# Linear attention on pairs of chunks: neighbouring tokens in one partition, 384-byte packets, a new order of work

## The chip, the cores and the metric

The kernel runs on one core of a Trainium2 chip. The metric is the device time of one execution in microseconds (us), lower is better. The engines are TensorE (PE), VectorE (DVE), ScalarE (ACT), GpSimd (POOL) and SyncE (SP); SP only issues transfers here, and 16 DMA engines carry them.

## The reference

Two stages follow one another: a linear attention with a decaying state, and a gated convolution over the whole sequence. B = 4 sequences, H = 8 heads, S = 768 tokens, D = 48 values a head, so 384 channels.

```python
for t in range(S):                                   # per batch and head
    cur = einsum('bhd,bhe->bhde', u[None] * kt, vt)
    y[:, :, t] = einsum('bhd,bhde->bhe', rt, state + cur)
    state = wt[:, :, :, None] * state + einsum('bhd,bhe->bhde', kt, vt)
x = y.transpose(0, 2, 1, 3).reshape(B, S, H * D)
x1, x2, x3 = split(x @ w_proj, 3)                    # w_proj [384, 1152]
x2_conv = irfft(rfft(x2, axis=1) * rfft(filter_fft, axis=0))
out = (x1 * x2_conv * x3) @ w_out                    # [4, 768, 384] float32
```

The inputs `r`, `k`, `v` and `w` are float32 of shape [4, 8, 768, 48], so one token of one head is 192 contiguous bytes.

## The kernel before

Stage one works on 24 chunks of 128 tokens, six for each sequence. A chunk has its 128 tokens in the 128 partitions. Chunks are loaded in groups of one or two (`group`): tiles `wl` (w), `kr` (k and r) and `vl` (v). One load brings one chunk of one input with a packet of 192 bytes for each token and head; 12 of the 24 chunks of v come through POOL's queue and are cast to bf16 on the way.

Per group, ACT takes the logarithm of w (`ln`, tile `lg`), and POOL or DVE makes the term of the current token: `rk` (r times k), `ru` (times u), `rh` (its two halves of 24 added), `cc` (the sum over a head, on DVE), and `vc` (v times that sum).

Per chunk (`first`), the steps are named with the chunk's number behind them: `cs` sums the logarithms over tokens as matmuls with triangular masks; `ex` takes the exponential of both sums; `kq` multiplies them with k and r (DVE); `ph` is the decay over the chunk; `tr` and `qk` turn the scaled k and r so that channels lie in partitions (PE and a copy, or a DMA transpose issued by SP for the last eight chunks); `sc` are the scores; `mt` copies them out of PSUM through the causal mask and `mc` cuts them on POOL where ACT copied them whole; `kv`, `ki` and `su` carry the state on (tile `S`); `yi`, `ys` and `y` add up the output in PSUM: the current token, the state, the scores. `xn` copies the output, `yt` and `xT` turn it.

Stage two (`second`) follows for each sequence: gate projections `p` and `q`, the side projection `xw`, the discrete Fourier transform by matrices `F` (`f`), the product with the filter's spectrum (`u`, `p`), the inverse transform `E` with its sums and differences (`aE` on DVE or `aw` on POOL, then `dE`), the gate (`yE`) and the output projection `o` with its copy `co` and store `so`. The matrices `F` and `mi` are sines that ACT makes with another function table (`trig`, `sin`, `is`, `table`).

The order of the work on all engines is one written-out list, `ORDER`: a line has the step, the engine's letter (P, A, D, G for POOL, S for SP, others for variants, `-` for a step left out) and a PSUM bank where one is needed. Each engine runs its lines in this order, and waits where data or a buffer is not ready. Lines `warm` are matmuls without use that keep PE running.

```python
op(f"l{name}{i}", [SP], lambda ...: nc.sync.dma_start(
    out=t[:, q], in_=x[b, :, rw, :].rearrange("h t d -> t h d")), ...)          # 128 partitions x 8 packets of 192 bytes
nc.tensor.matmul(p[:, par, j, :], qk[f][p0:p0 + D, j, :], qk[f][p0:p0 + D, HP + j, :], ...)   # sc: 8 a chunk, 128 columns
```

Of the kernel before, what the change touches and what calls it, by code (L numbers as in the profile page):

```python
# [20 lines left out]
L = 128  # L21
# [4 lines left out]
DP = 64  # L26
# [10 lines left out]
ADD, DVE2, ACT2, POOL2, FOLD, WIDE = "V", "M", "N", "C", "Q", "X"  # L37

NLW, NLD, NG, NF, NS, NX, NO = 3, 4, 3, 4, 3, 3, 4
CASTS = (2,4,6,8,10,12,)  # L40
NV, NVL = 6, 3
NTURN = 8
# [6 lines left out]
warm 16 4  # L49
first A  # L50
imaps G
smalls D
zeros D
pads D
signs D
lw0 S
lw3 S
kz1 D
ln0 A
maske G  # L60
lw2 S
lr0 S
u S
maskn G smalls
maps G
ang2 D
ia0.0 G
ia1.0 G
maski G
kz0 G pads  # L70
ang1 D
ang0 D
ia2.0 D
cs0 P 2
lk0 S
ln2 A
ex0 A
ew0 -
kq0 D
warm 8 0  # L80
warm 6 1
cs3 P 0
ex3 -
ia2.1 D
kw0 -
lw1 S
ur A
warm 4 5
um P 6
warm 5 5  # L90
tr0 P 4
lk3 S
lr3 S
ew3 X
lr1 S
lk1 S
kz2 G
ph0 A
ub A
ln1 A  # L100
lv0 S
rk0 G ang0
kz3 G kq0
ru0 G
rh0 D
cc0 D
qk0 A
kq3 -
kw3 G rh0
lv2 G cc0  # L110
warm 3 5
cs1 P 5
warm 3 7
sc0 P 3
mt0.1 D
mc0.1 -
lr2 S
lk2 S
vb0 G
vc0 G rh0  # L120
ex1 A
ph3 A
mt0.0 D
ew1 -
lv3 G
warm 3 7
cs2 P 0
warm 4 7
tr3 P 4
ex2 A  # L130
kq1 D
qk3 A
kw1 -
warm 2 7
tr1 P 7
mc0.0 -
rk1 D
ru1 D
rh1 G rk1
qk1 D  # L140
ph1 A
warm 3 2
sc3 P 4
kv0 P 2
su0 D
ew2 -
kq2 D
kw2 -
lv1 S
warm 2 3  # L150
sc1 P 6
yi0 P 2
y0 P
mt1.1 D
lw4 S
mt3.1 -
xn0 A
xa0 -
mt3.0 N
ph2 A  # L160
rk2 D
ru2 D
rh2 G rk2
vb1 A
tr2 P 3
warm 3 2
ki1 P 5
warm 2 2
kv1 P
lw5 S  # L170
lk4 S
lr4 S
qk2 A
ln3 A
mt1.0 D
cc1 D
yt0 P 2
lr5 S
lk5 S
lv5 S  # L180
warm 3 4
sc2 P 0
su1 D
warm 1 3
ki2 P 5
kv2 P
cc2 D
su2 D
cs4 P 6
ex4 A  # L190
wproj1 G
mc3.1 -
ki3 P 4
kv3 P
mt2.1 A
mc1.1 -
ia0.1 G
vc1 D
xT0 D
warm 2 3  # L200
yi1 P 2
ys1 P
vc2 G
mt2.0 D
mc1.0 -
y1 P
ew4 -
su3 D
mc2.1 G mt1.0
kq4 D  # L210
mc2.0 -
cs5 P 0
xn1 A
ex5 A
warm 1 4
yi2 P 3
ys2 P
y2 P
kw4 -
kq5 D  # L220
ew5 -
lw7 S
ph4 A
xn2 A
tr4 P 6
xa1 -
xa2 -
kw5 -
qk4 D
yt1 P 3  # L230
tr5 P 2
yi3 P 6
qk5 D
yt2 P 4
ph5 A
wproj0 G kq4
mc3.0 C
lv4 S
xT2 D
ys3 P  # L240
lr7 S
y3 P
xn3 D
sc4 P 4
mt4.0 D
xa3 -
trig A
sin2 A
rk3 G qk4
ru3 G qk5  # L250
warm 1 0
yt3 P 7
xT1 D
mt4.1 A
ia1.1 G mt4.0
warm 3 0
sc5 P 5
mt5.1 -
lw6 S
mt5.0 M  # L260
xw0.0 P 0
rh3 D
cc3 D
vb3 G rh3
sin1 A
vc3 G mt5.0
ki4 P 2
cxw0.0 D
xT3 A
warm 1 3  # L270
xw0.2 P 6
sin0 A
kv4 P
is A
cxw0.2 D
su4 D
warm 5 4
p0.2.0 P 5
p0.0.0 P 0
table A  # L280
lr6 S
lk6 S
lk7 S
mc4.1 G
filt S
lw8 S
lw9 S
cp0.0.0 D
yi4 P 6
yi5 P 2  # L290
ys5 P
lv7 G cxw0.2
mc5.0 -
mc5.1 -
ys4 P
y5 P
lk9 S
lk8 S
mc4.0 -
y4 P  # L300
xn4 D
if1 A
ln4 A
xn5 A
lv8 S
cs6 P 0
xa5 -
yt5 P 3
if0 A
ex6 A  # L310
lr9 S
xa4 -
yt4 P 2
xT5 D
xT4 D
cs7 P 6
ew6 -
kq6 D
ex7 A
ew7 -  # L320
xw0.4 P 2
lr8 S
kq7 D
ph6 A
cxw0.4 A
sd0.1.0 D
kw7 -
sd0.0.0 D
rk4 G
p0.2.1 P 4  # L330
cp0.2.1 A
ph7 A
kw6 -
lw10 S
p0.0.1 P 0
tr7 P 3
qk7 D
fsd0 D
fsd1 D
tr6 P 7  # L340
ru4 D
cp0.0.1 A
qk6 A
cp0.2.0 A
lv9 S
f0.2 P 0
cf0.2 A
sc6 P 6
mt6.1 -
mc6.1 -  # L350
mt6.0 N
f0.0 P 4
sc7 P 2
cf0.0 A
warm 2 0
h1 P 0
ln5 A
lv6 G sd0.1.0
h2 P 6
rh4 G fsd1  # L360
mt7.1 -
mt7.0 M
mc7.0 -
hc1 A
mc7.1 -
cc4 D
h0 P 2
hc2 A
kv6 P 4
hg1 D  # L370
hg2 D
hc0 A
cs8 P 0
su6 D
mc6.0 C
vc4 G
warm 2 5
yi6 P 6
y6 P
ex8 A  # L380
ew8 -
hg0 D
xn6 A
yi7 P 4
ys7 P
y7 P
xn7 A
xa7 -
xa6 -
cs9 P 6  # L390
kq8 D
yt6 P 3
ki7 P 2
kv7 P
su7 D
wproj2 G
yt7 P 4
xT7 D
ex9 A
xT6 A  # L400
kq9 D
kw8 -
rk5 G
ph8 A
ru5 D
rh5 D
cc5 D
ew9 -
tr8 P 5
ki8 P 2  # L410
qk8 A
ph9 A
vb5 G xT7
vc5 G
xw1.0 P 0
cxw1.0 A
kw9 -
tr9 P 3
qk9 A
kv8 P  # L420
sc8 P 4
su8 D
mt8.1 -
lw11 S
f0.1 P 0
ki9 P 6
kv9 P
mt8.0 M
if2 A
lk10 S  # L430
lk13 S
mc8.0 -
cf0.1 A
sc9 P 2
su9 D
q0.2.1 P 7
lr10 S
mt9.0 N
lk11 S
lr11 S  # L440
mt9.1 -
mc9.1 -
q0.0.1 P 5
lr13 S
yi9 P 0
q0.2.0 P 4
yi8 P 2
xq0.0.1 -
u10.0 D
lw12 S  # L450
ys9 P
ln6 A
ys8 P
cq0.0.1 D
lw13 S
mc8.1 -
y8 P
lv11 G su9
mc9.0 C
warm 5 2 192  # L460
y9 P
cs10 P 5
lr12 S
lv12 S
xq0.2.1 -
u00.0 D
xq0.2.0 -
xn8 A
xn9 A
q0.0.0 P 2  # L470
cq0.2.0 D
cq0.2.1 D
xq0.0.0 -
xa8 -
lk12 S
lv10 G
rk6 G
cq0.0.0 D
xa9 -
gq0.0.0 -  # L480
yt9 P 4
ex10 A
xT9 A
ru6 D
kq10 D
yt8 P 7
xT8 A
cs11 P 0
ex11 A
if3 A  # L490
kq11 D
warm 1 4
xw1.2 P 2
ew10 -
kw10 -
lk15 S
lv13 S
rh6 G ru6
cc6 D
ph10 A  # L500
lr15 S
gq0.2.0 -
lw15 S
lr14 S
p1.2.0 P 4
tr10 P 7
p1.0.0 P 5
cxw1.2 A
qk10 A
ew11 -  # L510
kw11 -
ph11 A
cp1.2.0 A
cp1.0.0 A
tr11 P 2
q1.0.0 P 0
ki10 P 3
sc10 P 4
xq1.0.0 -
ln7 A  # L520
p0.0 D
lw14 S
mt10.1 A
gq0.0.1 -
qk11 D
sc11 P 6
kv10 P
lv15 G
mt11.0 A
vc6 G  # L530
mc10.1 G kq11
mc11.0 G qk11
q1.2.0 P 2
xq1.2.0 -
cq1.0.0 D
mt10.0 D
mt11.1 D
cs12 P 0
rk7 G qk11
ru7 G  # L540
yi10 P 4
ex12 A
ew12 -
su10 D
lv19 G qk11
ys10 P
mc10.0 -
y10 P
lv14 G
mc11.1 -  # L550
cs13 P 6
gq0.2.1 -
cq1.2.0 D
kq12 D
xn10 A
ex13 A
yi11 - 2
ys11 P
y11 P
lk14 S  # L560
xn11 V
E0.0 P 4
kq13 D
ew13 -
kw13 -
ph12 A
gq1.2.0 -
vb7 A
xa10 -
kw12 -  # L570
tr12 P 0
lw17 S
lw16 S
rk8 G
cE0.0 A
aE0.0.1 D
ru8 G
yt10 P 1
E0.1 P 2
xT10 D  # L580
aE0.0.0 D
aw0.0.0 -
qk12 A
ph13 A
xa11 -
cE0.1 A
kv12 P 1
su12 D
aE0.1.0 D
tr13 P 7  # L590
E0.2 P 4
qk13 A
cE0.2 A
aE0.1.1 D
aw0.1.1 -
yt11 P 0
ki13 P 1
kv13 P
lk16 S
aw0.1.0 -  # L600
rh7 D
sc13 P 2
ln8 A
aw0.0.1 -
xT11 D
su13 D
sc12 P 6
mt12.0 N
aE0.2.0 D
aE0.2.1 D  # L610
mt13.1 D
mc13.1 -
mc12.0 C rh7
lv16 S
lw19 S
p1.0.1 P 0
mt12.1 -
cs14 P 4
xw1.4 P 6
dE0.0.1 -  # L620
mt13.0 D
q1.0.1 P 2
cp1.0.1 A
p1.2.1 P 1
cc7 D
ex14 A
kq14 D
ew14 -
kw14 -
tr14 P 0  # L630
cxw1.4 A
ln9 A
cq1.0.1 D
sd1.0.0 D
cp1.2.1 A
ph14 A
qk14 A
xq1.0.1 -
ki14 P 6
q1.2.1 P 7  # L640
vc7 G sd1.0.0
cs15 P 2
kv14 P
sd1.1.0 D
rh8 G
su14 D
lr16 S
lk17 S
# [1400 lines left out]
```

## Time and profile before

| | |
|---|---|
| time, median of 3 runs | 158.19 us (158.12 to 158.54) |
| the profiled execution | 157.08 us, of which its span 155.3 us |
| instructions in the profile | 4220 |
| busy: PE, DVE, ACT, POOL | 142.3, 135.5, 117.5, 102.0 us |
| moved by DMA | 27.12 MB in 112534 packets, 108545 of them under 512 bytes |
| mean granted clock of PE | 0.982 |

The span runs from the first instruction to the last of one profiled execution. Busy time counts instructions in progress; matmuls overlap and their ends are modelled, so PE's figure is not its array's use. A wait is put down to whatever came last. In the lists of instructions below, a name such as `kq_89` is one buffer of the tile `kq`.

### The profile page before, as it was taken

The page shows a single profiled execution, that of the slowest core. Times are in us where ns is not written, and L with a number is a line of the kernel's source. Part 1 is how long each engine was busy: PE and PEld are TensorE (multiplying, and loading weights), DVE is VectorE, ACT ScalarE, POOL GpSimd, SP SyncE. Part 2 cuts the span into 40 slices and gives each one's busy share as a digit, 9 for nine tenths or more (in the row PEclk, how much of TensorE's full clock was granted, in tenths as well). Part 3 has the DMA queues.
Part 4 walks back from the last instruction along what each step waited for, and adds up shares of the span by engine and source line. Part 5 has one row for each costly group of instructions (what it writes and reads, how often), then busy time and mean ns, then how long its engine had stood idle before and what let it go on. Part 6 is the DMA issues. An engine that isn't in the chain of part 4 may idle for free.

```text
span 155.3 us, 4220 instructions
## 1 busy us (share of the span) xinstructions
PE 142.3 (92%) x1634; PEld 89.4 (58%) x1634; DVE 135.5 (87%) x258; ACT 117.5 (76%) x195; POOL 102.0 (66%) x106
## 2 busy tenths in 40 slices
PE   7999894999999999999799999999999997999860
PEld 2455554656646767666566676665666664666430
DVE  4849984696999998999999999999999988799950
ACT  4584774897899894999879989989965575667650
POOL 6679595968229479589957988678796650802600
PEclk9999999699999999999999999999999999999997
DMA  5999999979999999899999918999997535000784
GB/s 105 227 212 218 194 145 215 200 135 339 177 187 213 198 181 180 142 199 176 187 192 201 179 25 144 220 193 189 178 183 149 155 122 209 0 0 34 294 330 159
DMA packets 112534, 27.12 MB, mean 175 GB/s; under 512 B 108545, under 2 KB 111106, under 8 KB 112514
## 3 DMA queue, kind: packets, MB, share of 16 engines
q1 hardware_dynamic: 98434, 24.49, 73.9%
q0 software_dynamic: 14080, 2.36, 20.0%
q8 instruction: 13, 0.21, 0.6%
q14 instruction: 7, 0.06, 0.1%
HBM read 22.41 MB, written 4.72 MB: 175 GB/s over the span
## 4 chain that ended last, share of the span: by engine, by line
PE 65%; DVE 11%; DMA 9%; ACT 4%; SPq 4%; issue 2%; DVEq 0%; ACTq 0%
PE banks L1768 13%; PE banks L1655 10%; PE banks L1380 7%; PE banks L1809 6%; PE banks L1950 5%; DMA kr<-in_k_dram 4%; PE banks L1865 4%; PE banks L1501 4%; SPq L1438 4%; PE banks L1519 4%; PE banks L1597 3%; DMA w<-in_w_dram 3%; DMA xT<-xn 3%; PE banks L1589 2%; PE banks L1473 2%
## 5 line engine op out<-in xcount | busy, mean ns | idle before, releaser
L1768 PE MATMUL banks<-xT,wproj 128*128 128x384 bf16 x144 | 27.3, 326 | 1.1 <-DVE xT L1334 1.0
L1328 DVE TENSOR_TENSOR kq<-banks,kr 128x768 bf16<-128x768 f32 x23 | 21.6, 950 | 3.1 <-DMA kr<-in_k_dram 2.7
L1328 POOL TENSOR_TENSOR vc<-vb,cc 128x768 bf16<-128x768 bf16 (+1 forms) x12 | 18.7, 1562 | 6.0 <-DVE sd L1820 3.1
L1328 POOL TENSOR_TENSOR rk<-kr 128x768 bf16<-128x768 f32 (+1 forms) x11 | 19.5, 1773 | 4.1 <-DMA kr<-in_k_dram 2.1
L1332 ACT ACTIVATE x<-banks 128x768 bf16<-128x768 f32 (+1 forms) x26 | 17.5, 687 | 5.2 <-PE banks L1809 3.0
L1482 ACT ACTIVATE banks<-banks 128x768 f32<-128x768 f32 x23 | 18.2, 798 | 1.9 <-PE banks L1476 1.6
L1535 DVE TENSOR_TENSOR mt<-banks,mask_excl 128x512 bf16<-128x512 f32 (+1 forms) x24 | 18.1, 772 | 1.3 <-PE banks L1519 1.1
L1768 PEld LDWEIGHTS <-wproj 128*128 128x128 bf16 x144 | 13.5, 98 | 9.3 <-issue 1.2
L1380 PE MATMUL banks<-wt 128*128 128x512 bf16 (+1 forms) x56 | 16.9, 397 | 1.1 <-DVE scl L1394 1.1
L1809 PE MATMUL banks<-wproj,xT 128*128 128x384 bf16 x72 | 13.7, 326 | 1.5 <-DMA xT<-xn 1.0
L1435 POOL DMA_DIRECT2D vb<-in_v_dram x12 | 11.3, 938 | 4.6 <-DVE sd L1820 3.3
L1540 POOL TENSOR_SCALAR_AFFINE_SELECT mt<-mt 128x512 bf16<-128x512 bf16 (+1 forms) x14 | 11.6, 834 | 3.5 <-ACT mt L1332 3.5
L1950 PE MATMUL banks<-wout,y 128*128 128x384 bf16 x72 | 13.3, 326 | 0.7 <-DVE y L1328 0.4
L1655 PE MATMUL banks<-sd,F 128*128 128x384 bf16 (+1 forms) x96 | 13.7, 328 | 0.0
L1501 PE MATMUL banks<-ident,kq 128*128 128x128 bf16 x144 | 11.1, 222 | 2.6 <-DVE kq L1328 2.1
L1332 ACT ACTIVATE qk<-banks 128x1024 bf16<-128x1024 bf16 x12 | 12.3, 1023 | 1.1 <-PE banks L1501 0.9
L1444 ACT ACTIVATE lg<-w 128x768 bf16<-128x768 f32 (+1 forms) x13 | 10.4, 798 | 3.2 <-DMA w<-in_w_dram 3.1
L1455 POOL TENSOR_TENSOR rk<-rk 128x384 bf16<-128x384 bf16 (+1 forms) x8 | 7.4, 921 | 7.7 <-DVE rk L1328 7.6
L1332 ACT ACTIVATE X<-banks 128x768 bf16<-128x768 f32 x12 | 9.8, 815 | 3.0 <-PE banks L1655 2.9
L1501 PEld LDWEIGHTS <-kq 128*128 128x128 bf16 x144 | 9.0, 98 | 4.9 <-DVE kq L1328 2.9
L1655 PEld LDWEIGHTS <-F 128*128 128x128 bf16 (+1 forms) x120 | 8.4, 103 | 5.6 <-issue 1.0
L1328 DVE TENSOR_TENSOR U<-X,hh 128x2304 bf16<-128x2304 bf16 (+1 forms) x12 | 11.6, 982 | 0.0
(118 smaller groups left out, 338.3 us busy)
## 6 DMA issues: line engine op xcount, KB each, us to landing
w<-in_w_dram SPq DMA_DIRECT2D x24, 192.0 KB, 4.2
kr<-in_r_dram SPq DMA_DIRECT2D x24, 192.0 KB, 4.5
kr<-in_k_dram SPq DMA_DIRECT2D x24, 192.0 KB, 4.5
out_dram<-o SPq DMA_DIRECT2D x9, 384.0 KB, 2.9
v<-in_v_dram SPq DMA_DIRECT2D x12, 192.0 KB, 4.0
vb<-in_v_dram POOLq DMA_DIRECT2D x12, 96.0 KB, 5.5
U<-in_moe_filter_fft_dram SPq DMA_DIRECT2D x1, 1152.0 KB, 6.0
wproj<-in_moe_w_proj_dram POOLq DMA_DIRECT2D x3, 288.0 KB, 5.1
```

The lines of the kernel that those rows point to most:

```text
L1328: return eng(e).tensor_mul(o, a, b)
L1332: return nc.scalar.activation(out=o, in_=a, func=AF.Copy)
L1380: nc.tensor.matmul(banks[:, at, lo:hi], wt[:, 0:L], x, start=True, stop=True)
L1435: op(f"lv{i}", [POOL], lambda e, bk, q=q, rw=rw: nc.gpsimd.dma_start(out=vb[fv][:, q], in_=v[b, :, rw, :].rearrange("h t d -> t h d")), w= ...
L1482: return nc.scalar.activation(out=o, in_=x, func=AF.Exp)
L1501: nc.tensor.transpose(p[:, HP * m + j, :], kq[f][:, m, 2 * j:2 * j + 2, :], ident)
L1535: return copy(ACT, o, x) if e in (ACT, ACT2) else nc.vector.tensor_mul(o, x, _mid(mask_excl, z - HP * a))
L1540: return nc.gpsimd.affine_select(out=o, in_=o, pattern=[[0, z - HP * a], [1, L]], compare_op=ALU.is_gt, fill=0.0, base=0, channel_multipli ...
L1655: nc.tensor.matmul(p[rows], F[:, ti, c0 + rows.start:c0 + rows.stop], x[q][:, ti, :], start=(ti == 0), stop=(ti == NT - 1),)
L1768: nc.tensor.matmul(p, wproj[:, cb, col0:col0 + L], xT[bx][:, cb, sl], start=(cb == 0), stop=(cb == CB - 1),)
L1809: nc.tensor.matmul(view(bk)[:, z], xT[bx][:, cb, (c0 + z) * L:(c0 + z + 1) * L], wproj[:, cb, C:2 * C], start=(cb == 0), stop=(cb == CB - 1),)
L1950: nc.tensor.matmul(view(bk)[:, z], yt_[:, z, :], wout[:, cb, :], start=(cb == 0), stop=(cb == CB - 1),)
```

## The change

Stage one now works on 12 pairs of chunks, three for each sequence. In a pair, partition p holds the tokens 2p and 2p + 1 of 256, so that one packet of k, r or v is two neighbouring tokens of a head, 384 bytes. Partitions 0 to 63 are then the first chunk (x = 0), 64 to 127 the second (x = 1), and a "slot" j = 0 or 1 is the even or the odd tokens of both. The decays w are still loaded chunk by chunk, in packets of 192 bytes.

- The masks of `cs` have 64 columns for each slot, and the two chunks' sums go to the two halves of the partitions.
- Scores, state and outputs use parts of the array: `sc` has 16 matmuls for a slot (64 columns instead of 128), `kv` 32 for a pair, `y` 32 for a pair with 64 rows each. A new step `yx` adds what the state gives in the other half of the rows. `yi` is done for all pairs.
- The tokens of a chunk then stand in the order even, odd in `xn` and `xT`; the angles of `F`, the inverse matrix `mi` and the filter's load follow that order, and the output projection writes 64 partitions at a time, so that the stores stay as they were.
- Where ACT copies the scores, POOL now cuts them by a product with a mask instead of a select by position.
- `rh` can be left out, and is in 8 of 12 groups; `cc` then sums all 48 values. The exponential into a float32 tile for POOL (`ew`, `kw`) and the copy with an addition (`V` for `xn`) are gone.
- `qk` and `xT` may be turned by DMA anywhere. The new order does so for chunks 12 to 23 and for the outputs of groups 3, 6, 8, 9 and 11. One load of v is cast on POOL's queue.
- `ORDER` is new as a whole: ACT makes the sines ahead of the first logarithm, and the `warm` lines stand in the start alone.

```diff
-            for name, t, x in (("w", wl[sw], w), ("k", kr[sl][:, 0], k), ("r", kr[sl][:, 1], r), ("v", vl[gi % NVL], v)):
...
+        def pair(x):
+            return x[b, :, rows, :].rearrange("h (p j) d -> p h j d", j=2)
...
+            op(f"l{name}{gi}", [SP], lambda e, bk, m=m, t=t: nc.sync.dma_start(out=kr[sl][:, m], in_=pair(t)),
+               w=[f"{name}.{sl}"])
...
+                for a, m in enumerate((mask_neg, mask_excl)):
+                    for x in (0, 1):
+                        nc.tensor.matmul(p[part[x], a, 0:C], m[:, j, :], lg[fg][:, x, :, 0:D], start=True, stop=True)
...
+            def turn_qk(e, bk):
+                if e == SP:
+                    for x in (0, 1):
+                        nc.sync.dma_start_transpose(
+                            out=qk[gi % NQ].rearrange("p (b x) (j t) -> p b x j t", x=2, j=2)[:, :, x, j],
+                            in_=kq[f][part[x]].rearrange("p a h d -> p (a h d)"))
...
+                for a in range(HP):
+                    for par in (0, 1):
+                        p0 = DP * par
+                        for x in (0, 1):
+                            nc.tensor.matmul(
+                                p[part[x], par, a, :], turned(bk, p0, 0, x, a, j), both(bk, p0, x, a),
+                                start=True, stop=True,
+                            )
...
+        def kvc(e, bk):
+            for j in (0, 1):
+                for h in range(H):
+                    for x in (0,) if final else (0, 1):
+                        nc.tensor.matmul(
+                            kvp(bk, x)[part[h % 2], h // 2, :], kq[fk[j]][part[x], 0, h, :], vb[fv][part[x], h, j, :],
+                            start=(j == 0 and h < 2), stop=(ci + x == 0 and j == 1 and h >= H - 2),
+                        )
...
+        def across(e, bk):
+            for a in range(HP):
+                for j in (0, 1):
+                    for x in (0, 1):
+                        p0 = DP * (1 - x)
+                        nc.tensor.matmul(
+                            yat(bk, x)[part[j], 2 * a + 1 - x, :], turned(bk, p0, 1, x, a, j),
+                            state(x)[p0:p0 + D, a, :], start=(a == 0), stop=False,
+                        )
...
+        def yy(e, bk):
+            for j in (0, 1):
+                for h in range(H):
+                    for x in (0, 1):
+                        nc.tensor.matmul(
+                            yat(bk, x)[:, h, :], mt[fs[j]][part[x], HP * (h % 2) + h // 2, :], vb[fv][part[x], h, j, :],
+                            start=False, stop=(j == 1 and h == H - 1),
+                        )
...
-                            nc.tensor.matmul(
-                                view(bk)[:, z], yt_[:, z, :], wout[:, cb, :],
-                                start=(cb == 0), stop=(cb == CB - 1),
-                            )
+                            for x in range(n):
+                                o, lo = (view(bk)[:, z], 0) if n == 1 else (view(bk)[DP * x:DP * x + DP, z], L * x + DP * z)
+                                nc.tensor.matmul(
+                                    o, yt_[:, lo:lo + L // n], wout[:, cb, :], start=(cb == 0), stop=(cb == CB - 1))
...
-first A
...
-lw0 S
+lr2 S
...
+warm 46 7
```

More of the change, by code (lines that the diff above doesn't have):

```diff
@@ new lines @@
+ang2 D
+warm 28 7
+um P 0
+ia1.0 G
+ia1.1 D
+signs D
+ia0.0 G
+lw2 S
+lw0 S
+lk2 S
+lk1 S
+ia2.1 D
+rk0 G
+smalls D
+ub D
+kz2 D
+ru0 G
+rh0 G
+ia0.1 D
+rk2 D
+lw1 S
+maske G
+ru2 D
+first A
+trig A
+sin0 A
+sin2 A
+is A
+sin1 A
+table A
+lr1 S
+cc0 D
+lw3 S
+rh2 D
+kz1 G
+lv0 S
+lw4 S
+maskl G
+lv2 S
+lw5 S
+lv1 S
+lk3 S
+rk1 G rh2
+cc2 D
+ru1 G
+ln0.1 A
+ln0.0 A
+warm 46 7
+cs0 P 0
+ex0 A
+kq0 D
+cs1 P 2
+warm 4 7
+tr0 P 4
+lw7 S
+ex1 A
+ln1 A
+cs3 P 6
+kq1 D
+ex3 A
+qk0 D
+lw6 S
+cs2 P 2
+ex2 A
```

2368 lines of the change are left out of this document (1059 added, 1309 removed).

## The prediction

> **What bounds the kernel now.** I read the page first (busy shares, slices, DMA queues, chain), then the windows by stage, then the chain of waits in order of time, and last the groups by form for prices.
>
> The page's lines on busy time, on DMA in 40 slices of 3.88 us, on the two data queues, and on the chain's engines:
>
> ```profile
> PE 142.3 (92%) x1634; PEld 89.4 (58%) x1634; DVE 135.5 (87%) x258; ACT 117.5 (76%) x195; POOL 102.0 (66%) x106
> ...
> DMA  5999999979999999899999918999997535000784
> GB/s 105 227 212 218 194 145 215 200 135 339 177 187 213 198 181 180 142 199 176 187 192 201 179 25 144 220 193 189 178 183 149 155 122 209 0 0 34 294 330 159
> ...
> q1 hardware_dynamic: 98434, 24.49, 73.9%
> q0 software_dynamic: 14080, 2.36, 20.0%
> ...
> PE 65%; DVE 11%; DMA 9%; ACT 4%; SPq 4%; issue 2%; DVEq 0%; ACTq 0%
> ```
>
> No engine is idle. The DMA engines are 90% busy or more in nearly every slice up to slice 32; the two queues' packets take 73.9 + 20.0 = 93.9% of the span, 145.8 us, at only some 190 GB/s while small packets run. The dip to 25 GB/s in slice 24 is taken up below. The windows, cut where I found the pace to change (columns: window, length, busy us and instructions of PE, weight loads, DVE, ACT, POOL, then granted clock, DMA share, GB/s):
>
> ```profile
> 0.00:12.00 12.00, 10.85 (x68) 5.11 (x69) 7.34 (x39) 7.28 (x12) 8.62 (x26) 1.00 0.93 182
> 12.00:26.00 14.00, 11.44 (x169) 6.99 (x167) 11.27 (x21) 8.65 (x15) 11.35 (x14) 1.00 1.31 193
> 26.00:38.50 12.50, 11.67 (x140) 7.80 (x141) 9.76 (x18) 10.54 (x15) 9.81 (x8) 0.86 0.98 221
> 38.50:100.00 61.50, 60.08 (x765) 40.07 (x766) 59.52 (x93) 54.73 (x95) 44.52 (x37) 1.00 1.12 175
> 100.00:130.00 30.00, 29.22 (x367) 18.27 (x365) 29.28 (x48) 22.87 (x39) 20.75 (x16) 1.00 0.90 171
> 130.00:155.30 25.30, 19.08 (x129) 11.20 (x129) 18.29 (x45) 13.39 (x21) 7.02 (x7) 0.96 0.37 141
> ```
>
> From 38.5 to 130 us DVE is busy 88.80 of 91.5 us (97%). PE reads as full too, but its ends are modelled. I take DVE as the pace there. Ahead of 38.5 us DVE is busy only 28.37 us, and after 130 it has gaps. The chain says what holds the first stretch, and where DMA comes back (start, length, what):
>
> ```profile
> 18.69 6.65 DMA kr<-in_k_dram
> 25.46 0.97 DVE kq L1328
> ...
> 102.78 3.92 DMA w<-in_w_dram
> ...
> 126.44 3.90 DMA xT<-xn
> ```
>
> DVE's timeline has the first and the seventh product `kq`, and ACT's what lies between:
>
> ```profile
> 7.35 0.96 DVE L1328 TENSOR_TENSOR kq<-banks,kr 128x768 bf16<-128x768 f32 x1 [0.36 <-DMA kr<-in_k_dram]
> ...
> 38.48 1.82 DVE L1328 TENSOR_TENSOR kq<-banks,kr 128x768 bf16<-128x768 f32 x2
> ```
>
> ```profile
> 7.00 0.50 ACT L1332 ACTIVATE u_r<-u_f 1x384 bf16<-1x384 f32 x1
> ...
> 26.63 1.28 ACT L1666 ACT_TABLE_LOAD   x1
> ```
>
> So chunk 0 is scaled at 7.35 us, but chunk 5 waits for its keys until 25.46, and chunks 6 and 7 stand behind ACT's sine block that begins at 26.63 and go at 38.48. That is the marker I use: DVE has done 28.37 us of work when chunk 6 begins. Later the chain loses 3.92 us to one load of `w` and 3.90 us to one transpose of `xn`.
>
> **The change, part by part.** Prices, from the groups by form (line, engine, operation, shapes, count | busy us, mean ns of one | idle before it):
>
> ```profile
> L1328 DVE TENSOR_TENSOR kq<-banks,kr 128x768 bf16<-128x768 f32 x23 | 21.6, 950 | 3.1 <-DMA kr<-in_k_dram 2.7 <-ACT banks L1482 0.2
> L1482 ACT ACTIVATE banks<-banks 128x768 f32<-128x768 f32 x23 | 18.2, 798 | 1.9 <-PE banks L1476 1.6
> L1535 DVE TENSOR_TENSOR mt<-banks,mask_excl 128x512 bf16<-128x512 f32 x20 | 13.2, 682 | 0.4 <-PE banks L1519 0.4
> L1570 DVE TENSOR_TENSOR S<-banks,phi 128x192 bf16<-128x192 f32 x20 | 7.0, 350 | 0.4 <-ACT lg L1444 0.2
> L1458 DVE TENSOR_REDUCE cc<-rk 128x16 f32<-128x384 bf16 x11 | 6.0, 545 | 0.1
> L1535 DVE TENSOR_TENSOR mt<-banks,mask_excl 128x1024 bf16<-128x1024 f32 x4 | 4.9, 1221 | 0.9 <-PE banks L1519 0.7
> L1908 DVE TENSOR_TENSOR y<-ev,banks 128x384 bf16<-128x384 f32 x9 | 4.9, 546 | 0.6 <-ACT ev L1332 0.6
> L1609 DVE TENSOR_TENSOR xn<-banks,vc 128x384 bf16<-128x384 f32 x8 | 4.3, 553 | 0.8 <-PE banks L1597 0.7
> L1334 DVE COPY qk<-banks 128x1024 bf16<-128x1024 bf16 x6 | 4.1, 683 | 0.3 <-PE banks L1501 0.3
> L1672 ACT ACTIVATE F<-o,mpi 128x768 bf16<-128x768 uint16 x3 | 2.8, 931 | 0.0
> L1661 ACT ACT_TABLE_LOAD x1 | 1.3, 1283 | 0.8 <-PEq L2033 0.8
> L1672 ACT ACTIVATE mi<-U,mpi 128x1152 bf16<-128x1152 uint16 x1 | 1.2, 1249 | 0.0
> L1444 ACT ACTIVATE lg<-w 128x384 bf16<-128x384 f32 x2 | 1.1, 530 | 1.5 <-DMA w<-in_w_dram 1.5
> ```
>
> *DMA.* Keys, queries and values come in 35 issues of 1,024 packets of 384 bytes, where 60 issues of 1,024 packets of 192 bytes stood; 11 of 12 cast loads (1,024 packets each) leave POOL's queue for SP's, and are counted in the 35 pair by pair. The packet price of the first queue is 0.739 x 155.3 x 16 / 98,434 = 18.7 ns; that of the second 0.200 x 155.3 x 16 / 14,080 = 35.3 ns. A 384-byte packet is not in the trace: at least one packet's price, at most two. Casts: -11,264 x 35.3 / 16 = -24.9 us of DMA time. The rest: -25,600 x 18.7 / 16 = -29.9 us to +11.8 us. So 13 to 55 us less of 145.8, before more transposes; I take 25, since the tenth slice, in which the filter's long packets land, moves 339 GB/s: a packet's cost is not all bytes. DMA then has slack. This alone is worth only what DVE waited for it; what is late next is DVE's and PE's own work.
>
> *The start.* ACT now makes the sines before the first logarithm. In its own queue, before and then after (`lg` logarithms, `banks` exponentials, `F` and `mi` sines):
>
> ```order
> L1661 LoadActFuncSet
> L1444 Activation lg_71<-w_61 128x8x48
> L1444 Activation lg_73<-w_63 128x16x48
> L1482 Activation banks<-banks 128x2x384
> L1332 Activation u_r<-u_f 1x384
> ```
>
> ```order
> L1130 LoadActFuncSet
> L1130 Activation u_r<-u_f 1x384
> L1524 LoadActFuncSet
> L1529 LoadActFuncSet
> L1535 Activation F<-o_128,mpi 128x768
> L1535 Activation F<-o_130,mpi 128x768
> L1535 Activation mi<-U,mpi 128x6x192
> L1535 Activation F<-o_129,mpi 128x768
> L1579 LoadActFuncSet
> L1261 Activation lg_71<-w_61 128x8x48 x2
> L1312 Activation banks<-banks 128x2x384 x2
> ```
>
> Four table loads (the first runs while `u` is under way), four sines and the row `u_r` now stand ahead of the first `lg`. `u_r` waits for `u`, the second load now instead of the fifth:
>
> ```profile
> 3.47 0.48 SPq L1409 DMA_DIRECT2D u_f<-in_u_dram  x1
> ```
>
> It was issued at 3.47 and used at 7.00, so it lands 3.5 us after issue at most; issued near 1.7 it is there by 5.2. Then u_r 0.50, two tables 2 x 1.283, sines 3 x 0.931 + 1.249, a table 1.283, two `lg` 2 x 0.530, sums about 0.4, one exponential 0.798: the first `kq` at about 15.9 us, 8.5 later than now. From there to chunk 6 DVE has 6 `kq` (0.950), 4 `qk` (0.683), masks 0.682 + 4 x 1.221, 5 `S` (0.350), one `cc` (0.545): 16.3 us, plus about 1.3 waiting for ACT, whose queue to the second turned chunk (four exponentials and some 2.9 us more) ends near 21. Chunk 6 begins at 33.5 instead of 38.48, since the sines and loads no longer stand between. DVE has done about 27.8 us then, some 11.5 of it ahead of the first `kq`. Its queue there, before and then after (`kq` tiles of chunks 4 and 5 at the end, `mt` masks, `S` states):
>
> ```order
> L1535 TensorTensor mt_105<-banks,mask_excl 128x512
> L1570 TensorTensor S_106<-banks,phi_96 128x192
> L1328 TensorTensor kq_89<-banks,kr_67 128x16x48
> L1328 TensorTensor kq_90<-banks,kr_67 128x16x48
> L1334 TensorCopy qk_99<-banks 128x1024
> L1334 TensorCopy qk_100<-banks 128x1024
> ```
>
> ```order
> L1379 TensorTensor mt_98<-banks,later 128x1024
> L1379 TensorTensor mt_101<-banks,later 128x1024
> L1423 TensorTensor S_104<-banks,phi_91 128x192
> L1276 TensorReduce cc_78<-rk_75 128x16
> L1126 TensorTensor kq_87<-banks,kr_66 128x16x48
> L1126 TensorTensor kq_88<-banks,kr_66 128x16x48
> ```
>
> Before, chunks 4 and 5 come after half a mask; after, two whole masks stand ahead of them, work that needs no later load. Bounds for this term: -9 us if ACT never holds DVE, +3 if a load or `u` is late by the 6.65 us that a key load cost; I take **-5.0 us**.
>
> *DVE's work.* Masks: 9 halves and 14 wholes for 20 and 4, 23.2 us for 18.5: +4.7. `cc`: in 8 of 12 groups DVE sums all 48 products; a row twice as long than the 545 ns one, between 0.545 and 1.09, I take 0.94: +3.0. The sums and differences `y` in PSUM: 14 at 0.55 for 24, -5.4, given to POOL. `xn`: one on DVE at 0.553 for ten, -4.8, given to ACT in pieces twice as wide. Products `rk`: -2.7. All smaller groups, counted alike: +2.5. Together **-2.7 us** of 135.45 (bounds -8 to +4). ACT and POOL come out within 3 us of their 117.5 and 102.0 by the same count and keep their slack. From chunk 6, DVE has 132.8 - 27.8 = 105.0 us left where it had 107.1. It now takes 116.8 us of time for those, 9.7 with no DVE work. So the span is 33.5 + 105.0 + 9.7 = 148.2 us, if nothing new waits.
>
> *PE.* 2,500 matmuls instead of 1,634 by the lists. The chain has the prices:
>
> ```profile
> 36.11 0.30 PE banks L1589 x16
> ...
> 54.07 0.24 PE banks L1560 x8
> 54.64 1.10 PE banks L1655 x12
> ...
> 83.41 2.06 PE banks L1655 x12
> ...
> 97.83 0.36 PE banks L1560 x16
> ```
>
> Two matmuls in different parts of the array run together: 16 of `S,qk` in 0.30 us is 19 ns each, and 12 with half the columns take 1.10 us where 12 full ones take 2.06. Splitting a matmul into halves thus costs the array about nothing, if four quarters also run together, which no row shows. What comes on top is the `yx` matmuls, `yi` on all chunks and the starts of runs: eight `vb,kq` take 0.24 and sixteen 0.36, so 0.12 us a run is fixed. With fewer transposes taken off, I count +2.5 us; bounds -3 (only the transposes count) to +16 (866 more at 19 ns). The Trainium skill (TensorEngine Tiling (Array Packing), Key Properties) says that a change of tiling mode drains the array. The fixed 0.12 us bears that out, and the longer runs of the new kernel pay it less often per matmul. PE stands beside a full DVE, so I add the **+2.5** in full.
>
> *SP.* `qk` of chunks 12 to 23 and `xT` of six groups are turned by DMA: 34 issues for 11. SP's queue at the first of them, before and then after (`qk` turned from `kq`; the rest loads):
>
> ```order
> L1438 DMACopy kr_66<-in_k_dram 128x8x48 x2
> L1507 DmaTransposeAnt qk_100<-kq_90 128x8x128
> L1438 DMACopy w_63<-in_w_dram 128x8x48
> L1438 DMACopy kr_67<-in_r_dram 128x8x48
> L1438 DMACopy kr_67<-in_k_dram 128x8x48
> ```
>
> ```order
> L1245 DMACopy w_63<-in_w_dram 128x8x48 x2
> L1335 DmaTransposeAnt qk_96<-kq_88 128x8x64 x2
> L1335 DmaTransposeAnt qk_96<-kq_87 128x8x64 x2
> L1245 DMACopy w_61<-in_w_dram 128x8x48
> L1251 DMACopy v_69<-in_v_dram 128x8x96
> ```
>
> Loads of `w` and `v` that stood behind one transpose now stand behind four. Each waits for a `kq` of DVE; the wait of before (columns: waiter, releaser, total us, times, longest):
>
> ```profile
> SPq L1507 <- DVE kq L1328: 5.7, 1, 5.7
> ```
>
> 5.7 us of SP emptied the queue (slice 24), and the chain paid 3.92 us for `w` 15 us later. Deeper slack in DMA hides a part; bounds -3.9 (even that one goes) to +12, taken **+1.0**.
>
> Sum: 148.2 + 2.5 + 1.0 = 151.7 us of span, against 155.3. The profiled execution took 157.08, 1.78 more than its span, and the median of the runs 158.19 is 1.11 above that: 151.7 + 2.9 = **154.6 us**.
>
> **The rivals.**
> (a) *SP's queue is the new wait: slower.* Two more waits for `kq` that empty the loads as in slice 24, each 3.92 us on the chain: 154.6 + 7.8 = 162.4. One such echo leaves 158.5, no change; the second decides. For it: three times the transposes, in the same queue as the loads. Against it: 13 to 55 us less packet time. Chance 0.20, and 0.07 for no change.
> (b) *The quarters do not run together: slower.* If half of the 866 extra matmuls cost 19 ns, PE gains 8.2 us instead of 2.5; at all of them 16.5. PE reads 60.08 of 61.5 us busy, so it would take over: 160.3 to 168.6. Chance 0.16. By the Trainium skill (TensorE: Matmul & The Clock Gate, on the issue floor) no two matmuls start closer than about 25 ns; the 19 ns here contradicts it. By that rule the price would be 21.7 us and the time 173.8; the row leaves it no chance of its own.
> (c) *DMA's slack closes DVE's gaps too*: the 3.92 and 3.90 us go as well and DVE runs without holes: 154.6 - 6 = 148.6. For it: both are DMA waits. Against: DVE was full beside the first. Chance 0.09.
>
> **How the numbers follow.** The forecast with its own range of 150.5 to 157.7 has 0.44; 0.04 lies just above it. Faster by over 0.3% (0.5 us, about what a measurement of this kernel can tell from none): 0.44 + 0.09 = 0.53. Same 0.07. Slower 0.20 + 0.16 + 0.04 = 0.40. The range takes (c) in and reaches into (a) and (b), to 165.
>
> **What would show it.** Right: first `kq` near 16 us, chunk 6 near 33, DVE near 97% until 125, DMA slices under 9 after the start, no load of `w` in the chain past 40. Wrong: a chain with `SPq` waits for `kq` and slices of DMA near empty while ACT waits for `w` (a); PE in the chain on scores and `kv` at 30 ns a piece or more with DVE idling (b); chunk 6 later than 38 us would break the first term.

## The result and the profile after

| | before | after |
|---|---|---|
| time, median | 158.37 us (158.12 to 159.13) | 221.86 us (220.75 to 227.32) |
| the profiled execution's span | 155.3 us | 219.8 us |
| mean granted clock of PE | 0.982 | 0.851 |

The changed kernel is slower: 1.397 times the time before, 95% interval 1.389 to 1.406. The forecast was 154.6, and its range ended at 165. This ratio, and the ratios below, leave out runs that fell in a slower state of the chip (here the one of 227.32).

The page of after: busy time; PE's clock and the DMA share in 40 slices of 5.5 us; the two data queues; the chain's engines.

```profile
PE 161.9 (74%) x2500; PEld 104.7 (48%) x2500; DVE 139.8 (64%) x231; ACT 116.1 (53%) x172; POOL 99.4 (45%) x96
...
PEclk9975758997967995879955999559999879699999
DMA  6999999989140591059701469999435211006065
...
q1 hardware_dynamic: 81282, 28.52, 56.0%
q0 software_dynamic: 2640, 1.38, 5.2%
...
PE 41%; ACT 17%; DVE 14%; issue 7%; DMA 2%; SPq 1%; DVEq 0%; ACTq 0%
```

The work is nearly the same, the time is not. DVE does 139.8 us of work for 135.5 and is idle for 80.0 us of the span instead of 19.8: of the 64.5 us, 4.3 are work and 60.2 are holes. PE, ACT and POOL have holes too, and DMA slices read 0 and 1, so no engine is full. The chain goes less over PE and more over ACT and DVE; DMA and SP's queue carry 3% of it, for 13% before. (It begins at 34.99 us; what came earlier is not traced, so its shares add up to 82%.)

Two windows of after, then one of before, with the columns of the windows shown earlier:

```profile
80.00:100.00 20.00, 11.52 (x219) 8.50 (x220) 12.36 (x15) 8.98 (x15) 4.70 (x4) 0.74 0.43 91
100.00:120.00 20.00, 12.12 (x152) 7.87 (x150) 9.02 (x14) 8.62 (x13) 8.65 (x5) 0.75 0.48 110
```

```profile
80.00:100.00 20.00, 19.88 (x269) 13.64 (x268) 19.35 (x32) 18.77 (x35) 15.11 (x13) 1.00 0.91 153
```

In 20 us before, DVE worked 19.35 us; after, 12.36 and 9.02. The chain of after in that stretch shows what fills the time (start, length, what; `qk` and `X` are ACT's copies, L1365 the scores, `mt` the masked copy, `S` the state, L1460 the scores' part of `y`, `lg` the logarithm):

```profile
79.37 0.07 ACT qk L1130
79.44 0.85 issue
80.29 0.81 ACT X L1130
81.11 0.04 issue
81.15 0.44 PE banks L1365 x16
81.64 0.04 issue
81.68 1.29 DVE mt L1379 x2
82.97 0.86 DVE cc L1276
83.83 0.28 DVE S L1423
84.15 0.69 PE banks L1365 x16
84.86 0.57 issue
85.43 0.56 DVE g L1661
...
86.44 1.39 PE banks L1445 x16
...
88.80 0.64 PE banks L1460 x32
89.44 0.46 PE banks L1301 x4
...
90.68 0.83 ACT lg L1261
91.52 0.70 ACT banks L1312
```

The end of each piece lets the next one begin on another engine: ACT, PE, DVE, PE, DVE, PE, ACT. While one works, the others wait, each behind its own next line. Among the 195 longest pieces of the chain, rows `issue` left out, the engine changes 85 times; in before's, 31 times. The waits add up accordingly (waiter, releaser: total us, times, longest):

```profile
ACT x L1130 <- PE banks L1676: 17.2, 9, 3.3
...
DVE kq L1126 <- ACT banks L1312: 16.0, 14, 3.1
...
DVE mt L1379 <- PE banks L1365: 13.0, 10, 3.5
ACT x L1130 <- PE banks L1635: 12.9, 10, 3.4
ACT mt L1130 <- PE banks L1365: 12.9, 7, 3.8
...
ACT banks L1312 <- PE banks L1306: 11.3, 8, 3.9
```

There is no single large wait, but many of 1 to 2 us, in both directions between the same three engines. Four theories stood: the written order makes the engines take turns (order); the layout by pairs is dear in itself (pairs); SP's queue holds the loads up (SP); PE's clock, 0.851, is the loss (clock).

### The profile page after: what moved, and what is told of

It is laid out like the page before. It is cut to its first block, busy times and chain, and to the rows that moved or that the text cites. A ratio compares the mean times of both kernels' runs of the same rounds, so it can differ in the third digit from the quotient of the medians.

```text
span 219.8 us, 5865 instructions
## 1 busy us (share of the span) xinstructions
PE 161.9 (74%) x2500; PEld 104.7 (48%) x2500; DVE 139.8 (64%) x231; ACT 116.1 (53%) x172; POOL 99.4 (45%) x96
## 4 chain that ended last, share of the span: by engine, by line
PE 41%; ACT 17%; DVE 14%; issue 7%; DMA 2%; SPq 1%; DVEq 0%; ACTq 0%
PE banks L1635 9%; PE banks L1518 7%; PE banks L1676 6%; PE banks L1819 5%; ACT x L1130 4%; ACT banks L1312 4%; DVE mt L1379 4%; PE banks L1301 2%; DMA kr<-in_k_dram 2%; DVE g L1661 2%; PE banks L1365 2%; ACT lg L1261 2%; DVE kq L1126 2%; PE banks L1732 2%; PE banks L1328 2%
## 5 line engine op out<-in xcount | busy, mean ns | idle before, releaser
L1130 ACT ACTIVATE x<-banks 128x768 bf16<-128x768 f32 (+1 forms) x27 | 18.7, 703 | 30.1 <-PE banks L1676 17.2
L1379 DVE TENSOR_TENSOR mt<-banks,later 128x1024 bf16<-128x1024 f32 (+1 forms) x23 | 22.8, 1012 | 16.7 <-PE banks L1365 13.0
L1126 POOL TENSOR_TENSOR vc<-vb,cc 128x768 bf16<-128x768 bf16 x9 | 13.3, 1473 | 19.6 <-DVE cc L1276 9.9
L1126 POOL TENSOR_TENSOR rk<-rk,u_b 128x768 bf16<-128x768 bf16 x11 | 18.0, 1636 | 8.9 <-DVE sd L1687 7.4
L1384 POOL TENSOR_TENSOR mt<-mt,later 128x512 bf16<-128x512 bf16 (+1 forms) x8 | 12.1, 1515 | 16.3 <-ACT mt L1130 16.2
L1365 PE MATMUL banks<-qk 48*64 48x128 bf16 x384 | 9.9, 236 | 11.3 <-DVE S L1423 2.6
L1301 PE MATMUL banks<-lg,mask_neg 128*64 128x384 bf16 x48 | 10.1, 407 | 10.1 <-ACT lg L1261 6.2
L1518 PE MATMUL banks<-sd,F 128*64 128x384 bf16 (+1 forms) x96 | 14.8, 345 | 2.5 <-ACT X L1130 2.0
L1661 DVE TENSOR_TENSOR g<-banks,x 128x384 bf16<-128x384 f32 (+1 forms) x14 | 10.5, 754 | 9.6 <-PE banks L1635 6.7
L1819 PE MATMUL banks<-wout,y 128*64 128x384 bf16 (+1 forms) x138 | 13.6, 328 | 3.2 <-ACT x L1130 1.8
L1365 PEld LDWEIGHTS <-qk 48*64 48x64 bf16 x384 | 7.5, 115 | 14.6 <-issue 11.6
L1126 POOL TENSOR_TENSOR rk<-kr 128x768 bf16<-128x768 f32 x6 | 10.9, 1812 | 7.3 <-DVE sd L1687 5.9
```

What stands on the lines that cost most here:

```text
L1126: return eng(e).tensor_mul(o, a, b)
L1130: return nc.scalar.activation(out=o, in_=a, func=AF.Copy)
L1301: nc.tensor.matmul(p[part[x], a, 0:C], m[:, j, :], lg[fg][:, x, :, 0:D], start=True, stop=True)
L1365: nc.tensor.matmul(p[part[x], par, a, :], turned(bk, p0, 0, x, a, j), both(bk, p0, x, a), start=True, stop=True,)
L1379: return copy(ACT, o, x_) if e in (ACT, ACT2) else nc.vector.tensor_mul(o, x_, _mid(lat, HP * (z - a)))
L1384: return nc.gpsimd.tensor_mul(o, o, _mid(lat, HP * (z - a)))
```

## The experiments

Before was measured anew beside each group of experiments: 158.84, 158.96, 159.85 and 158.77 us; ratios are against these.

**Another order for the same work.** All steps and their engines stay; the lines stand in another order and take other PSUM banks. The list came from a random search over orders, each priced by replaying it with the durations of after's trace. A line of POOL can also name a step of DVE that it waits for even where it needs nothing from it, a tie (`rk1 G rh2`); after's list has 14 ties, the new one none.

```diff
-pads D
-kz0 G
+lw0 S
+lk0 S
... (the whole list)
```

> The changed kernel with the same steps on the same engines, but the list written anew: other order of the lines, PSUM banks given out anew, no ties. Order theory (the work itself is fine; the new list makes the engines wait for one another at hand-offs): 150 to 172 us, the busy times of PE, DVE, ACT and POOL within 8% of those of the changed kernel, idle time gone. Pairs theory (the paired layout is what costs: two-bank tiles held long, 64x64 parts, long chains in a pair): no order helps much, 205 us or more. SP theory (34 transposes in the queue of the loads): the transposes stay, so 200 us or more.

Measured: 185.97 us (185.46 to 188.91), ratio 1.170 (1.162 to 1.178). The order theory's range was missed upward, but 36 of the 63 us are gone with nothing done to the layout, which leaves the pairs and SP theories (205 us or more, 200 or more) without these 36. Busy time and chain:

```profile
PE 152.6 (83%) x2498; PEld 93.8 (51%) x2498; DVE 151.6 (82%) x231; ACT 116.5 (63%) x172; POOL 105.0 (57%) x96
...
PE 36%; DVE 23%; SPq 14%; DMA 11%; ACT 7%; issue 6%; ACTq 0%; DVEq 0%
```

The engine changes 29 times now, counted as before, no more often than in before's chain, and yet 27 us stand between them: the count is a sign, not a price. SP's queue and DMA, 3% of after's chain, are 25% of this one.

**SP's loads ahead of its transposes.** Only lines of SP move.

```diff
+lw1 S
 ia1.0 G
...
-lw2 S
-lw0 S
-lk2 S
```

> The changed kernel with only SP's lines moved: loads issued ahead of the transposes that they stood behind, as far as their buffers allow; all other engines keep their order. SP theory (prediction's rival a, the waits of SP for kq and xn empty the loads): 212 us or less, and the load of keys at about 130 us gone from the chain. Order theory and pairs theory: no change, 219 to 224 us, since in the trace the chain passes through a load only once after 50 us (4.68 us).

Measured: 222.86 us (220.48 to 224.22), ratio 1.392 (1.379 to 1.405). Nothing is gained: rival (a) is refuted for this order, though the empty DMA slices are what it had foretold. The load of keys at 131 us (4.68 us of after's chain) is gone from the chain between 120 and 140 us, as the SP theory said, and the time is none the shorter: other work ended just as late.

**The clock.** Matmuls without use are put where PE was idle, 302 units in one kernel and 109 in another; and before is run without the 77 units that it has in its body.

```diff
 xn2 A
+warm 15 0
 yt2 P 6
```

> The changed kernel with 302 units of matmuls without use put where PE idles by the trace, in banks that are free there. Clock theory (idle PE loses its clock, and half of the added time is matmuls at half clock): granted clock from 0.85 to 0.95 or more, time 200 to 208 us; what is left above 158 is not the clock. If the clock were a mere companion: time unchanged or longer, 220 to 230 us, whatever the clock.

> The changed kernel with 109 units of matmuls without use in PE's idle time (302 in e3, where they took 39 us of PE themselves), each filling some 40% of the gap. Clock theory: granted clock 0.92 or more and 205 to 215 us, so that some 10 us of the 63 are the clock's. Clock as a companion only: 219 us or more.

> The kernel before without the 77 units of matmuls without use that stand behind the first cs in its list. Clock theory as the whole cause (the change dropped these lines): granted clock falls toward 0.85 and the time rises by 15 us or more, to 173 or more. Order theory: PE of this kernel is busy anyway, so the clock stays above 0.95 and the time within 3 us of 158.4.

Measured: 231.81 us (230.6 to 232.4), ratio 1.459 (1.449 to 1.468); with fewer, 230.00 (228.67 to 231.41), 1.449 (1.438 to 1.460); before without them, 157.88 (155.40 to 160.34), 0.984 (0.974 to 0.994). The first:

```profile
PE 183.7 (80%) x2658; PEld 109.7 (48%) x2658; DVE 141.1 (62%) x231; ACT 115.8 (51%) x172; POOL 98.7 (43%) x96
...
PEclk9995789999997999999999899999999769999999
```

The clock rose to 0.947. PE's busy time less that of the useless matmuls fell from 151.1 to 131.9 us, but these took 51.8 us of PE instead of 10.8, and PE is in the chain all along. With fewer, the clock rose to 0.872 alone, short of the 0.92 that the test needed. Filling did not pay. How much the low clock itself costs is not shown by this: each such kernel pays for the filling as well. Before without its units was measured again:

> Before without the 77 units of useless matmuls in its body, measured in more rounds, since its first four runs lay between 155.4 and 160.3 us. If PE's short holes hide those matmuls wholly, the time is within 0.3% of before's own (157.9 to 159.1 us at before's usual 158.4). If the earlier ratio of 0.984 was real, 155 to 156.5. If they keep PE's clock up, as they seem meant to do, 160 or more with a granted clock near 0.92.

Measured: 155.96 us (155.63 to 156.99), ratio 0.986 (0.980 to 0.992), with the granted clock at 0.934. So before, too, pays about 2 us for matmuls that hold its clock up (0.982 with them); that the change drops them from the body is no part of the 63 us. This is the one kernel here below before's time, by 1.4%.

**A second list, with and without DMA's turning.** The second kernel also turns `qk` of chunks 12 to 23 and all of `xT` on PE, with copies on DVE and ACT.

```diff
-qk12 S
+tr12 P 4
...
+qk12 D
```

> As e1: the changed kernel with the same steps on the same engines, only the list and the banks written anew, now with what e1's trace showed taken into account: a keys load occupies the DMA engines 1.55 us and not 1.03, two transposes 1.7 us, and DVE's bf16 products run 1.5 to 2 times as long beside POOL. Order theory: below e1's 186, 165 to 180 us, DVE busy back from 151.6 toward 140. Floor theory (186 is what paired chunks cost under any order, by PSUM, DMA or DVE): 183 us or more.

> As the run before it, and besides qk of chunks 12 to 23 and the six xT that DMA turned are turned by PE and copied by ACT or DVE (12 x 16 and 6 x 6 to 12 more matmuls, 18 more copies of 0.5 to 1.0 us); banks and order written anew for that. Transposes as a cost of DMA time and of SP's queue: 16128 packets of 256 bytes and some 23 to 30 us of DMA time gone, the time 5 us or more below that of the run before it. Transposes hidden: within 3 us of it, or slower, since the copies come on top of DVE and ACT.

Measured: 187.82 us (185.64 to 188.96), ratio 1.176 (1.167 to 1.186), the order theory's range missed and the floor theory's met; without DMA's turning 179.23 (177.65 to 182.53), 1.123 (1.114 to 1.132), in spite of 126 more matmuls and 18 more copies. The 8.6 us between them cannot be put down to the 34 transposes alone: the two lists differ as a whole, three lists for the same steps lie 5 us apart (182.7 to 187.8), and in the chain of the first SP's queue and DMA have 1% (traced from 38.27 us on). Part of the miss of the first is one product on DVE, 7.71 us here and 1.35 at its next turn, beside a POOL that runs without a pause (timelines of DVE and of POOL; the rows `DMA_DIRECT2D` are POOL issuing a load):

```profile
106.89 7.71 DVE L1125 TENSOR_TENSOR U<-X,hh 128x2304 bf16<-128x2304 bf16 x1
...
121.72 1.35 DVE L1125 TENSOR_TENSOR U<-X,hh 128x2304 bf16<-128x2304 bf16 x1
```

```profile
106.55 0.81 POOL L1231 DMA_DIRECT2D wout<-in_moe_w_out_dram  x1
107.38 0.93 POOL L1664 TENSOR_TENSOR g<-xe,x 128x384 bf16<-128x384 f32 x1
108.26 1.48 POOL L1125 TENSOR_TENSOR vc<-vb,cc 128x768 bf16<-128x768 bf16 x1
109.69 1.63 POOL L1125 TENSOR_TENSOR rk<-rk,u_b 128x768 bf16<-128x768 bf16 x1
111.28 1.14 POOL L1383 TENSOR_TENSOR mt<-mt,later 128x512 bf16<-128x512 bf16 x1
112.37 0.94 POOL L1254 DMA_DIRECT2D vb<-in_v_dram  x1
113.33 2.76 POOL L1125 TENSOR_TENSOR rk<-rk,u_b 128x768 bf16<-128x768 bf16 x1
```

**Banks alone, and a third list.** First, after's lines stand as they are and 73 of 177 bank numbers change. Second, a new list in which 10 ties hold POOL behind those DVE products.

```diff
-tr0 P 4
+tr0 P 5
```

> The changed kernel with its list line for line, but 73 of its 177 PSUM bank numbers given out anew, so that a step takes a bank that has been read out earlier. Bank theory (most of the waits are for the wrong bank): 205 us or less. Order theory (the order of the steps makes the waits, the numbers follow): 213 to 219 us.

> As e1 and e5 (same steps, same engines, DMA turning kept), the list written anew a third time, from what e5 showed: POOL's lines are held back behind DVE's products, sums and differences in bf16 (a product of 1.35 us took 7.71 us beside POOL in e5), and matmuls are counted at half speed after a window of 3.4 us in which PE was busy under half. Order theory: 163 to 178 us, DVE busy back to 142 or less. Floor theory (paired chunks cost 180 us or more under any order): 181 us or more.

Measured: 219.99 us (218.20 to 223.09), ratio 1.382 (1.367 to 1.397): about 2 us less than after, which is not clear of the two intervals, so the bank numbers are worth little. The third list: 182.73 (180.74 to 183.86), 1.144 (1.127 to 1.161), the order theory's range missed again and the floor theory's met, though DVE's work came back as expected:

```profile
PE 152.4 (84%) x2498; PEld 95.6 (53%) x2498; DVE 140.2 (77%) x231; ACT 117.0 (65%) x172; POOL 99.2 (55%) x96
```

DVE's work is that of after (139.8 us), and its idle time is 41.1 us instead of 80.0: with the same steps, on the same engines, at the same price, the list alone makes this difference.

**The control: before's own work, reordered in the same way.** Three lists had stopped at 183 to 188 us. Either the new layout keeps some 25 us, or lists of this make do. So before's own steps were put through the same search, starting from its own list. The list that came out has none of the 41 ties of before's list and none of its 77 useless matmul units in the body.

```diff
-kq0 D
-warm 8 0
-warm 6 1
-cs3 P 0
... (the whole list)
```

> A control for e1, e5 and e9: the kernel before, its steps on the same engines, its list and banks written anew by the same procedure as theirs, starting from its own list; its warm lines only at the start. If the procedure writes lists as good as the one that the kernel before has: 150 to 160 us, and what e9 lies above that is the layout's. If its lists are worse by their own: 165 us or more, and e1 to e9 above 158 are no evidence against the paired layout.

Measured: 184.62 us (183.53 to 184.96), ratio 1.162 (1.152 to 1.172).

```profile
PE 151.2 (83%) x1598; PEld 92.8 (51%) x1598; DVE 150.1 (82%) x258; ACT 118.2 (65%) x195; POOL 103.5 (57%) x106
```

The old layout under such a list takes 184.6 us, 25 more than its own list; the new one took 186.0 and 187.8 under lists without ties, and 179.2 where DMA turns nothing. So what these lists lie above 158 is no evidence against the layout: the procedure alone costs the old layout as much. Two things cost it: DVE is idle for 32.6 us instead of 19.8, and its work takes 150.1 us instead of 135.5, since without ties more of its bf16 products run beside POOL (six products `U` take 11.9 us for 8.5). The third list for the new layout (182.7) had ties and so is not matched by this control. It is one control of one procedure; a list for the new layout as good as before's was not found, no kernel with the new layout beats before, and what the layout itself costs or saves stays open.

**The sines late.** Only ACT's sine block moves, back behind `ex5`.

```diff
-trig A
-sin0 A
... (to table A)
 ex5 A
+trig A
+sin0 A
```

> The changed kernel with its four sines and two table loads on ACT moved from ahead of the first logarithm to behind the exponentials of chunk 5, where they stood in the kernel before. The prediction's first step (sines first are worth 5.0 us): 225 to 229 us, first kq 6 us or more earlier than 15.64, chunk 6 later than 38.97. If the hand-offs behind it swallow the start's difference: 220 to 224 us.

Measured: 226.97 to 233.36 us in four runs, too far apart for a ratio; the lowest is 5.1 above after's median. The lowest lies in the range foretold for sines worth 5 us and the others above it, but the way there was another. In the profile (ACT, then DVE) the first logarithm waited for `w`, so that the first `kq` was no earlier, and chunk 6 came 8.0 us later than in after:

```profile
12.76 0.94 ACT L1261 ACTIVATE lg<-w 128x384 bf16<-128x384 f32 x2 [6.67 <-DMA w<-in_w_dram]
```

```profile
15.38 1.82 DVE L1126 TENSOR_TENSOR kq<-banks,kr 128x768 bf16<-128x768 f32 x2 [0.80 <-ACT banks L1312]
...
47.00 1.82 DVE L1126 TENSOR_TENSOR kq<-banks,kr 128x768 bf16<-128x768 f32 x2 [2.47 <-ACT banks L1312]
```

## Why the prediction was wrong, point by point

**The sum's frame: the step that failed.** "So the span is 33.5 + 105.0 + 9.7 = 148.2 us, if nothing new waits." It took DVE as the pace because DVE was busy 97% of the time in before, and carried that pace into an order that was new as a whole. In after, from chunk 6 on:

```profile
38.97:219.80 180.83, 130.37 (x2001) 85.09 (x1998) 114.73 (x165) 91.50 (x140) 68.40 (x51) 0.87 0.53 117
```

The span is 71.6 us longer than these 148.2. Chunk 6 came 5.5 us late, DVE's work behind it was 114.7 us instead of 105.0, and DVE's time without work behind it was 66.1 us instead of 9.7. So the term that failed is the 9.7, with "if nothing new waits" as its ground: it is 56.4 of the 71.6 us. The list made at least half of these holes: the third list keeps the steps, the engines and DVE's work, and DVE's idle time over the span falls from 80.0 to 41.1 us. That DVE was full was an achievement of before's list, not a property of the work: under the control's list, for the same steps, DVE is idle for 32.6 us instead of 19.8. What is left above before under the better lists, some 24 us, is not explained beyond the control. The shares of the chain (PE 65%, DVE 11%) could have warned, since a pace that DVE alone set would stand in the chain. None of the rivals had this case: each looked at one resource, the slower ones at SP's queue and at PE's array. A chance for "the new list makes the engines take turns" was missing. It could not be read from before's trace; but the lists of both kernels were there, and counting where PE's next line needs what DVE or ACT has yet to make would have asked the question.

**The start.** Markers in after, the first `kq` and chunk 6:

```profile
15.64 1.82 DVE L1126 TENSOR_TENSOR kq<-banks,kr 128x768 bf16<-128x768 f32 x2 [1.03 <-DMA v<-in_v_dram]
...
38.97 1.82 DVE L1126 TENSOR_TENSOR kq<-banks,kr 128x768 bf16<-128x768 f32 x2 [0.53 <-ACT banks L1312]
```

The first was put at 15.9, right to 0.3 us. Chunk 6 was put at 33.5 and came at 38.97, as late as before, the sign that was to break the first term. DVE's work between the two was 15.3 us, near the 16.3 of the sum; its idle time was 8.0 us instead of 1.3, of which its longer waits give 3.6 to ACT's exponentials, 2.4 to PE and 1.4 to POOL. The move of the sines does not test this term: with them late the first `kq` came no earlier, since the first logarithm then waited 6.67 us for `w`, whose load stands where it stood. What it shows is that in this list the late place is worse, by 5.1 us in the lowest run.

**DVE's work.** 139.8 us, not 132.8. Prices in after (count | busy us, mean ns | idle before):

```profile
L1126 DVE TENSOR_TENSOR rk<-kr 128x768 bf16<-128x768 f32 x6 | 7.9, 1309 | 3.4 <-DMA kr<-in_k_dram 3.4
L1276 DVE TENSOR_REDUCE cc<-rk 128x16 f32<-128x768 bf16 x8 | 7.5, 942 | 0.0
...
L1126 DVE TENSOR_TENSOR vc<-vb,cc 128x768 bf16<-128x768 bf16 x3 | 4.3, 1423 | 0.1
```

`cc` was put at 0.94 us and is 0.942. Masks, `cc`, `y` and `xn` came out as counted (+4.7, +3.0, -5.5, -4.9). What failed is the products: `rk` in all its forms fell by 0.5 us, not 2.7, since six of them take 1.309 us each where the price in before was 0.948, and `vc` on DVE rose from 0.6 to 4.3, more than all the +2.5 of the smaller groups. Seven us too few, against 60 of holes.

**PE.** The quarters do run together, against rival (b). One row of after and one of before, both at full clock, for the scores of one slot and of one chunk:

```profile
156.90 0.42 PE L1365 MATMUL banks<-qk 48*64 48x128 bf16 x16 [0.28 <-ACT o L1130]
```

```profile
44.46 0.40 PE L1519 MATMUL banks<-qk 48*128 48x128 bf16 x8
```

In the same way 32 matmuls of `y` take 0.56 us, where 16 of before took 0.57. The starts within a group of four scores lie 3 to 4 ns apart, as they do within before's pairs; the 16 of `y` in before, each on the whole array, start 25 to 26 ns apart but for the first. The sign that the prediction named for (b), 30 ns a piece or more on scores, does stand in the chain (0.69 us for 16), but where the clock was at half. Less the time of the useless matmuls, PE was busy for 125.4 us in before and 151.1 in after; with the clock at 0.947, in the kernel with 302 units, for 131.9. So some 19 of the 25.7 us more went with the clock, and some 6 are left for the +2.5 of the sum. (The fixed 0.12 us of a run in the prediction shows that a run has a cost of its own; no row tells whether a change of mode is what makes it.) The clock followed the holes: 12 matmuls of the transform take

```profile
64.84 4.01 PE banks L1518 x12
```

where 12 in before took 2.06 at full clock.

**SP.** Put at +1.0 with up to +12. In this order moving the loads was worth nothing. With DMA's turning taken out of a tighter one the time was 3.5 to 8.6 us lower, depending on which of the other lists it is set beside, so what the transposes cost there is not shown. (Before turned `qk` by DMA for six chunks, 17 and 19 to 23, not for its last eight; the 11 issues of the sum are right.)

**DMA.** The loads' packets and casts fell by 28.1 us of DMA time by the trace (109.1 to 81.0), where 25 was taken; the transposes added 12, other packets 5, and the total went from 145.8 to 134.5. The size was right in part by luck: both prices per packet were averages over long packets too, 18.7 ns where a packet of 192 bytes took 16.1, and 35.3 where a cast packet took 29.2. It was worth nothing, since the slack lies where no engine waits for DMA: rival (c) needed an order in which DVE is full.

## What to carry to other kernels

Where engines take their work in a written order, that order can weigh as much as any operation: here the same steps took 221.9 to 182.7 us. When it is rewritten, the pace of the old profile need not carry over, and "the order is worse" needs a chance and a price of its own. A busy share near 100% can say how good the list is, and not which engine bounds the work. Before blaming a new layout, put the old one through the same reordering: here the old one lost 25 us by it, so the like loss of the new one could not be laid to the layout. The control must leave out the same things, ties too.

## What the runs showed of the hardware

**PE's clock.** In all fourteen traces the granted clock is either 0.5 or 1.0, and changes on a grid of 3.41 us. After the first 12 us, 65 of 68 windows of this grid that followed one with PE busy under 50% were at half, and 348 of 364 that followed one at 90% or more were full; between 60 and 80%, 109 were full and 32 at half. The state before counts too: behind a window at full clock with PE busy 80% or more, no window fell to half (0 of 364, of which 83 behind 80 to 90%). The Trainium skill (TensorE: Matmul & The Clock Gate, "Part 1: The HAM clock gate (the "warmup" mystery)") gives half rate after at least one idle window of about 3.4 us. The length agrees with 3.41; that the window must be idle does not: under half busy was enough, and in after the longest pause of PE behind the first 12 us is 2.58 us. So a kernel with many short holes loses its clock without one pause as long as a window.

**DVE beside POOL.** The product of 1.35 us took 7.71 while POOL ran five operations of 0.93 to 2.76 us nearly end to end. The Trainium skill (SBUF — State Buffer, "SBUF: two separate sides") says that DVE and POOL lock a shared pair of ports for a whole instruction and that the loser blocks fully. The row agrees that one of them blocks. It shows more: DVE did not get its turn between several of POOL's instructions in a row, though its product began at 106.89 us, ahead of POOL's first of the five at 107.38 (spans on POOL are rough). Nor does all work of POOL do it: in before the same product took 1.39 us at 104.54 us, with POOL busy throughout on the end of a product from float32 and a cast.

**Packets.** By the trace, a packet of 384 bytes takes 24.2 ns of a DMA engine (35,840 of them, 54.3 us over the 16 engines), one of 192 bytes in before 16.1 ns (86,016, 86.7 us): twice the bytes for 1.5 times the time.
